# Expert rows of the last two experts: quarter-row gathers and 32x32 transposes on VectorE in place of TensorE's turns

## The chip, the cores and the metric

The kernel runs on one core of a Trainium2 chip. The metric is device time in microseconds of one execution, lower is better. Before the change the median of 3 runs is 857.68 us (857.0 to 857.93). The core has five engines with a queue of their own each, which run their instructions in order and wait for each other through semaphores: TensorE (PE; PEld is its weight load), VectorE (DVE), ScalarE (ACT), GpSimd (POOL) and SyncE (SP), which issues DMAs. Matmuls write to PSUM, from where VectorE or ScalarE take the results.

## The reference

Attention with a sigmoid in place of the softmax gives x; then a mixture of experts with a fixed capacity, in which each token goes to one expert of 8.

```python
scores = scale * np.matmul(q, k.transpose(0, 1, 3, 2)) - np.log(S)   # q, k, v: 8 x 12 x 448 x 64
attn = 1.0 / (1.0 + np.exp(-scores))
x = np.matmul(attn, v) ...                                           # as 3584 tokens x 768
logits = x @ w_gate                                                  # 768 x 8
# (token, expert) pairs in descending order of logit; a token takes the first
# expert that still has room; an expert takes 448 tokens
for e in range(E):
    mask = assigned == e
    h = np.maximum(x[mask] @ w1[e], 0.0)                             # 448x768 @ 768x1024
    out[mask] = h @ w2[e]                                            # 448x1024 @ 1024x768
```

## The kernel before

**Stages.** The attention part comes first (to about 300 us) and writes x to DRAM (`xs`). Then the eight experts follow one another, in the order in which the routing finds them; they are counted 0 to 7 here. Each expert has 448 tokens, in four blocks of 128, 128, 128 and 64 rows.

**Precision.** Matrix products run on a type of 32 bits that TensorE multiplies fast but rounded, so every operand is split into a rounded part and a rest (`wh`, `wl` for weights; `xh`, `xl` for rows; two halves of `hb` and `hr` for h), and three matmuls are added where one would do.

**An expert** (`moe`, a generator that yields after each matmul):
- the *first product*, 144 matmuls of 448 columns (L811 to L815): four quarters, each of two weight units. After each quarter ScalarE writes h twice, rounded (L821, `hb`, `hr`) and in full (L824, `h0`, which has two buffers), and GpSimd subtracts the one from the other (L827);
- the *second product*, 176 matmuls of 384 columns (L856), in two halves of four weight units each. ScalarE copies results out (L771 to L783), GpSimd adds a rest (L784), and after the second half four indirect DMAs on GpSimd's queue (L757) scatter rows to the output.

**Weights** come in 16 units per expert (units 0 to 127 in all): SyncE loads a unit (L698 for w1, L702 for w2, four buffers) three units ahead, ScalarE rounds it (L709), and a subtraction (L711) gives the rest, two units ahead. It runs on GpSimd, and for odd units from 96 on (experts 6 and 7) on VectorE.

**Rows.** A list (`listed`, tile `r_idx`) holds an expert's tokens. Four indirect DMAs on GpSimd's queue gather the rows into `xr` (L731). A *turn* (`xturn`) is then three 128x128 transposes on TensorE per half of the features (L745), ScalarE's rounded copy `xh` (L748) and VectorE's rest `xl` (L749). The first product of the next expert needs all of `xh` and `xl`.

**Routing** (`Router`) runs on VectorE beside the products: a search over bits for an expert's threshold (L178 to L287), a pick, then `place` (two matmuls, L333 and L334, on a running sum r_tot) and `lists` (a one-hot comparison L352, 32 matmuls L360, a cast L377, two matmuls L381, a conversion to the index tile L383). It takes place from expert 0 up to the second product of expert 5.

**Order.** It is written out by hand. A clock adds a cost in ns for each matmul (189 in the first product, 164 in the second); the loop over `moe(kx)` calls the next piece of routing or the first entry of a list of chores (gathers, turns, scatters: a due time each, a last expert by which it has to be done) when its time has come, with 1000 ns between two chores. `flush` issues at an expert's end, one behind another, all chores that are due by then. The order in which pieces are issued is the order in each engine's queue.

Of the kernel before, what the change touches and what calls it, by code (L numbers as in the profile page):

```python
# [21 lines left out]
XR_BUFS = 8  # L22
# [16 lines left out]
HOLD_NS = 600  # L39
H_POOL = 8  # L40
EARLY = 2
FIRST = 4000.0
W_DVE = 96

# [10 lines left out]
def route_consts(nc, cp, K):  # L55
# [47 lines left out]
    nc.vector.tensor_copy(t7, t5)  # L103
    nc.vector.tensor_scalar(K.SEL, t6, t7, None, OP.is_equal)
    K.kk = cp.tile([128, 16, 3], I32, name="c_kk")
    g = 0
# [14 lines left out]
class Router:  # L121
# [219 lines left out]

    def lists(self, alone):

# [36 lines left out]
        for h in range(2):  # L380
            nc.tensor.matmul(p[64 * h:64 * h + 64, :4], bt, K.SEL[:, h, :], start=True, stop=True)  # L381
# [28 lines left out]
    def phase(self, k):  # L410
        if k:
            self.remove()
        if k < 7:
            if k:
                yield T_KEY
                yield from self.keys()
            yield T_KT if k else T_KEYS
            yield from self.search(k == 0)
            yield T_KAP
            self.pick()  # L420
        else:
            self.left()
        yield T_PICK
        self.place(k == 0)
        yield from self.lists(k == 0)


def moe_attention(tc, q, k, v, w_gate, w1, w2, out):
# [7 lines left out]
    with contextlib.ExitStack() as ctx:  # L436
# [213 lines left out]
        late.pop(0)()  # L650
        picked, listed = {}, {}

        def routing():
            for kx in range(E):
                for t in R.phase(kx):
                    if kx not in picked and R.ei is not None:
                        picked[kx] = R.ei
                    yield t
                listed[kx] = R.idx
                R.ei = None  # L660
                yield 0
# [24 lines left out]
        def load_w(u, behind=False):  # L686
# [8 lines left out]
            if st == 0:  # L695
                t = t.rearrange("p (a f) -> p a f", a=3)
                src = w1[ds(gate[kx], 1)].rearrange("e (a p) f -> p (e a) f", p=128)
                nc.sync.dma_start(t, src[:, 3 * j:3 * j + 3, i * 256:(i + 1) * 256])  # L698
            else:
                t = t.rearrange("p (a f) -> p a f", a=2)  # L700
                src = w2[ds(gate[kx], 1)].rearrange("e (a p) f -> p (e a) f", p=128)
                nc.sync.dma_start(t, src[:, 2 * j:2 * j + 2, i * 384:(i + 1) * 384])  # L702
            raw[u] = t

        def split_w(u):
# [3 lines left out]
            nc.scalar.activation(hi, raw[u], AF.Copy)  # L709
            eng = nc.vector if u < 2 or (u >= W_DVE and u % 2) else nc.gpsimd  # L710
            eng.tensor_tensor(lo, raw[u], hi.bitcast(F32), OP.subtract)  # L711
# [22 lines left out]
        def xturn(kx, j, n, hf, wide):  # L734
# [13 lines left out]
            nc.scalar.activation(xh[sl], pv, AF.Copy)  # L748
            nc.vector.tensor_tensor(xl[sl], pv, xh[sl].bitcast(F32), OP.subtract)  # L749

        scat, chores = [], []
# [133 lines left out]
        for kx in range(E):  # L885
            turned = kx + 1 == E
            start = clock[0]

            def prepare():
                t0 = clock[0]  # L890
                lag = max(5000, min(14000, start + 40000 - t0))
                space = max(TURN_FIRST, min(TURN_NS, (start + EXPERT_NS - t0 - lag - 1000) // 4))
                for j, n in blocks():
# [22 lines left out]
            for step, cost in enumerate(moe(kx)):  # L916
# [56 lines left out]
```

## Time and profile before

| | |
|---|---|
| median of the runs | 857.68 us |
| the profiled execution | 857.27 us |
| its span, first to last instruction | 855.5 us |
| expert 5, first matmul to that of expert 6 | 67.16 us (659.08 to 726.24) |
| expert 6 | 62.81 us (726.24 to 789.05) |
| expert 7 up to its last matmul | 60.55 us (789.05 to 849.60) |
| turns on TensorE (L745) | 192 transposes |

All times of the profile come from one execution and are counted from its first instruction. A line of the page or of a view names the source line, the engine, the operation, the tile written and the tiles read, with their shapes; "idle before" is the time in which that engine did nothing ahead of the instruction, and behind the arrow stands what it waited for. "issue" means that it waited for nothing that the profile shows. The chain that ended last is followed back from the end, so its pieces are those which set the time.

### The profile page before, as it was taken

Reading aid. Unit: us, or ns where it says so; the run is one execution under the profiler, and the core shown is the slowest. Engines: PE = TensorE matmul, PEld = TensorE weight load, DVE = VectorE, ACT = ScalarE, POOL = GpSimd, SP = SyncE. Lnnn points to the kernel's source line nnn. Section 1 sums busy time; section 2 is a strip of 40 time slices with the busy share of each in tenths; the row PEclk is TensorE's granted clock in tenths of the full one; section 3 lists DMA queues with packets and bytes.
Section 4 is the critical chain, followed back from the end, with each engine's and each line's share of the span. In section 5 each row is a group of like instructions: output and inputs, shape, how many; then the busy total and the mean of one; then the engine's idle time right before and its main releaser. Section 6 shows DMA issues by size and latency. Waiting matters only on the chain.

```text
span 855.5 us, 16407 instructions
## 1 busy us (share of the span) xinstructions
PE 817.9 (96%) x5517; PEld 650.2 (76%) x5517; DVE 538.9 (63%) x2069; ACT 437.9 (51%) x603; POOL 484.4 (57%) x506
## 2 busy tenths in 40 slices
PE   6999999999999839999999999999999999999997
PEld 3455455454554728999988999999999989999996
DVE  4565555565554989977978969969879852321211
ACT  6777777778775833425424434434434424443332
POOL 9545444445410014867866866876875885743753
PEclk9999999999999978999999999999999999999999
DMA  9776666656530975345435353453553554443331
GB/s 177 153 153 128 131 129 130 124 118 138 121 65 2 318 254 158 111 138 175 114 106 170 115 147 131 147 169 101 157 166 103 156 156 161 139 129 112 129 103 64
DMA packets 196532, 117.58 MB, mean 137 GB/s; under 512 B 145248, under 2 KB 186208, under 8 KB 196448
## 3 DMA queue, kind: packets, MB, share of 16 engines
q1 hardware_dynamic: 183840, 83.30, 37.6%
q0 software_dynamic: 10752, 33.02, 12.6%
q8 instruction: 43, 0.70, 0.4%
q10 hardware_dynamic: 1856, 0.23, 0.2%
q14 instruction: 41, 0.34, 0.1%
HBM read 94.47 MB, written 22.02 MB: 136 GB/s over the span
## 4 chain that ended last, share of the span: by engine, by line
PE 85%; DVE 10%; issue 2%; DMA 1%; ACT 0%; POOL 0%; ACTq 0%; POOLq 0%; SPq 0%; DVEq 0%
PE sc L856 26%; PE tp L559 13%; PE sc L535 12%; PE sc L811 8%; PE sc L815 8%; PE sc L813 8%; DVE r_junk L178 4%; PE tp L565 3%; PE tp L745 2%; PE sc L545 2%; PE tp L580 1%; PE rt L360 1%; DVE r_j L272 1%; DVE r_T L281 1%; DMA xr<-xs,r_idx 1%
## 5 line engine op out<-in xcount | busy, mean ns | idle before, releaser
L711 POOL TENSOR_TENSOR wl<-wr,wh 128x768 fp32r<-128x768 f32 x110 | 202.3, 1855 | 28.3 <-ACT wh L709 28.0
L856 PE MATMUL sc<-wh,hb 128*128 128x384 f32 x768 | 199.8, 338 | 0.0
L525 ACT ACTIVATE at<-sc,bias 128x896 f32<-128x896 f32 x168 | 160.8, 1004 | 62.2 <-PE sc L545 37.8
L466 POOL DMA_DIRECT2D nkq<-in_q_dram x188 | 118.2, 640 | 114.5 <-DVE kqT L510 109.3
L813 PE MATMUL sc<-xl,wh 128*128 128x448 f32 (+2 forms) x396 | 144.2, 364 | 0.0
L811 PE MATMUL sc<-xh,wh 128*128 128x448 f32 (+2 forms) x396 | 144.2, 364 | 0.0
L815 PE MATMUL sc<-xh,wl 128*128 128x448 f32 (+2 forms) x396 | 143.9, 363 | 0.0
L856 PEld LDWEIGHTS sc<-wh,hb 128*128 128x128 f32 x768 | 138.3, 188 | 1.7 <-issue 0.6
L856 PE MATMUL sc<-wl,hb 128*128 128x384 f32 x384 | 130.8, 341 | 0.0
L709 ACT ACTIVATE wh<-wr 128x768 fp32r<-128x768 f32 x128 | 104.0, 850 | 50.9 <-PE sc L856 29.9
L178 DVE TENSOR_SCALAR_CACHE_REDUCE r_junk<-r_KE,r_T 128x224 bf16<-128x224 f32 x315 | 123.3, 442 | 0.1
L559 PE MATMUL tp<-at,nv 128*64 128x448 f32 x576 | 118.6, 548 | 0.0
L821 ACT ACTIVATE hb<-sc 128x768 fp32r<-128x768 f32 x32 | 26.0, 813 | 134.0 <-PE sc L815 134.0
L519 DVE TENSOR_TENSOR kqL<-kqT,kqH 128x896 fp32r<-128x896 f32 (+1 forms) x49 | 52.5, 1072 | 57.8 <-ACT kqH L517 57.7
L827 POOL TENSOR_TENSOR hb<-h,hb 128x768 fp32r<-128x768 f32 x32 | 59.1, 1848 | 50.4 <-ACT h L824 50.4
L559 PEld LDWEIGHTS tp<-at,nv 128*64 128x64 f32 x576 | 37.1, 136 | 59.4 <-issue 57.1
L813 PEld LDWEIGHTS sc<-xl,wh 128*128 128x128 f32 x396 | 74.6, 188 | 6.9 <-DVE xl L749 0.2
L815 PEld LDWEIGHTS sc<-xh,wl 128*128 128x128 f32 x396 | 74.6, 188 | 6.8 <-issue 0.2
L811 PEld LDWEIGHTS sc<-xh,wh 128*128 128x128 f32 x396 | 74.6, 188 | 6.6
L711 DVE TENSOR_TENSOR wl<-wr,wh 128x768 fp32r<-128x768 f32 x18 | 24.0, 1332 | 82.1 <-ACT wh L709 82.0
L856 PEld LDWEIGHTS sc<-wl,hb 128*128 128x128 f32 x384 | 72.2, 188 | 1.8 <-issue 1.0
L535 PE MATMUL sc<-kqH 64*128 64x448 f32 x288 | 59.8, 412 | 6.9 <-ACT kqH L517 6.9
(185 smaller groups left out, 1232.8 us busy)
## 6 DMA issues: line engine op xcount, KB each, us to landing
wr<-in_moe_w_dram SPq DMA_DIRECT2D x128, 384.0 KB, 3.3
xs<-xr SPq DMA_DIRECT2D x32, 336.0 KB, 4.7
nkq<-in_k_dram SPq DMA_DIRECT2D x190, 56.0 KB, 2.5
nkq<-in_q_dram POOLq DMA_DIRECT2D x188, 56.0 KB, 2.6
nv<-in_v_dram SPq DMA_DIRECT2D x94, 96.0 KB, 2.5
nr<-in_v_dram SPq DMA_DIRECT2D x48, 32.0 KB, 2.2
xr<-xs,r_idx POOLq DMA_INDIRECT x32, 4.6
out_dram<-yr,r_idx POOLq DMA_INDIRECT x32, 3.6
```

The costliest lines, as they stand in the source:

```text
L178: nc.vector.tensor_scalar(junk[:, a:b], self.KE[:, a:b], T[:, i:i + 1].bitcast(F32), None, OP.is_ge, OP.add, accum_out=cnt[:, i:i + 1])
L466: qn.dma_start(t[o:o + 32, n], rws[x])
L525: nc.scalar.activation(a, p[:, :, :S], AF.Sigmoid, bias=bias, scale=1 / math.sqrt(D))
L535: nc.tensor.matmul(p[:, j, :S], R[half, c * 128:(c + 1) * 128], M[half], start=i == 0, stop=i == 2)
L559: nc.tensor.matmul(p[j * 64:j * 64 + 64, :S], nat["v", b, g][:, h0 + j, c, :], AT[b, pr, c][:, j, :], start=(c == 0), stop=(c == 2 and pr ...
L709: nc.scalar.activation(hi, raw[u], AF.Copy)
L711: eng.tensor_tensor(lo, raw[u], hi.bitcast(F32), OP.subtract)
L811: nc.tensor.matmul(ph[:, f, lo:hi], wh[:, a, fs], xh[:, dd, lo:hi], start=st, stop=False)
L813: nc.tensor.matmul(ph[:, f, lo:hi], wh[:, a, fs], xl[:, dd, lo:hi], start=False, stop=False)
L815: nc.tensor.matmul(ph[:, f, lo:hi], wl[:, a, fs], xh[:, dd, lo:hi], start=False, stop=en)
L827: nc.gpsimd.tensor_tensor(h2, h0[:, :, t], h1.bitcast(F32), OP.subtract)
L856: nc.tensor.matmul(o, hs, w[:, a], start=st and n == 0, stop=en and n == len(terms) - 1)
```

## The change

For experts 6 and 7 (`BY_DVE`) the rows are not turned on TensorE any more.
- `lists` makes a second index tile `idq` for them: 8 small matmuls (L398) with a selection constant bring tokens to 32-partition groups, and one VectorE operation (L405) makes token * 4 + group of it.
- `gather_quarters` (L783): a gather fetches 128 quarter rows of 192 features: partition 32 g + r gets quarter g of token r of a group of 32 tokens. There are 14 gathers for an expert where there were 4.
- `vturn` (L794): VectorE's 32x32 block transposes, 128 x 384 at a time, write into PSUM what TensorE's transposes wrote; the copies to `xh` and `xl` stay. Feature 192 g + 32 a + w then stands on partition 32 g + w in chunk a, so the w1 rows are loaded in that order, by four DMAs of 32 partitions (L726).
- `FETCH` and `VTURN` set start and spacing of these chores. The turns of expert 6 are due from 7000 ns after its list on, those of expert 7 from 31000 ns after the start of expert 6, in its second product.
- The weight subtraction runs on VectorE for all units from 91 on (the fourth unit of the second product of expert 5).
- Two constants are made early (`SELG`, `gq`).

```diff
+BY_DVE = 6
+FETCH = {6: (0, 1000), 7: (18000, 2500)}
+VTURN = {6: (7000, 3800), 7: (31000, 3000)}
-W_DVE = 96
+W_DVE = lambda u: u >= 91
...
+        if quarters:
+            for u in range(2):
+                for g in range(4):
+                    nc.tensor.matmul(p[32 * g:32 * g + 32, 8 + 8 * u:16 + 8 * u], bt[:, 32 * u:32 * u + 32], K.SELG,
+                                     start=True, stop=True)
         idx = wk.tile([128, 4], I32, name="r_idx", bufs=4)
         nc.vector.tensor_scalar(idx, p[:, :4], 1792.0, None, OP.add)
+        if quarters:
+            self.idq = wk.tile([128, 8, 2], I32, name="r_idq")
+            nc.vector.tensor_scalar(self.idq, p[:, 8:24].rearrange("p (u s) -> p s u", u=2), 4.0, K.gq, OP.mult, OP.add)
...
+                    src = w1[ds(gate[kx], 1)].rearrange("e (g a p) f -> g p (e a) f", g=4, a=ND)
+                    for g in range(4):
+                        nc.sync.dma_start(t[32 * g:32 * g + 32], src[g, :, 3 * j:3 * j + 3, fs])
...
-            eng = nc.vector if u < 2 or (u >= W_DVE and u % 2) else nc.gpsimd
+            eng = nc.vector if u < 2 or W_DVE(u) else nc.gpsimd
...
+        def gather_quarters(kx, s):
+            j, i = s // 4, s % 4
+            if i == 0:
+                xg[kx, j] = xp.tile([128, DM], F32, name="xr", bufs=XR_BUFS)
+            nc.gpsimd.indirect_dma_start(out=xg[kx, j][:, 192 * i:192 * i + 192], out_offset=None,
+                                         in_=xs.rearrange("t (g w) -> (t g) w", g=4),
+                                         in_offset=bass.IndirectOffsetOnAxis(ap=quarter[kx][:, s // 2, s % 2:s % 2 + 1], axis=0))
+        def vturn(kx, j, n, hf):
...
+            p = ps_t.tile([128, 512], F32, name="tp")
+            v = xg[kx, j].rearrange("p (i w) -> p i w", w=192)[:, :n // 32, 96 * hf:96 * hf + 96]
+            nc.vector.transpose(p[:, :3 * n].rearrange("p (a i w) -> p a i w", a=3, w=32),
+                                v.rearrange("p i (a w) -> p a i w", w=32))
...
+            nc.scalar.activation(xh[sl], pv, AF.Copy)
+            return lambda: nc.vector.tensor_tensor(xl[sl], pv, xh[sl].bitcast(F32), OP.subtract)
+        def vturn_block(kx, j, n):
+            for rest in [vturn(kx, j, n, hf) for hf in range(2)]:
+                rest()
...
+            def fetch(e, t, due):
+                if e >= BY_DVE:
+                    for s in range(S // 32):
+                        chores.append((t + FETCH[e][0] + FETCH[e][1] * s, due, lambda s=s: gather_quarters(e, s)))
...
+                if kx + 1 >= BY_DVE:
+                    if kx + 1 not in fetched:
+                        fetch(kx + 1, t0, kx + 1)
+                    for j, n in blocks():
+                        chores.append((t0 + VTURN[kx + 1][0] + VTURN[kx + 1][1] * j, kx + 1,
+                                       lambda j=j, n=n: vturn_block(kx + 1, j, n)))
+                    return
...
-                    for j, n in blocks():
-                        chores.append((t + 1500 * j, kx + 1, lambda j=j, n=n, e=kx + 2: gather(e, j, n)))
+                    fetch(kx + 2, t, kx + 1)
```

What this moves in the queues is seen at three places. A row gives the source line (after, lines behind the top of the file stand lower), the operation, the tile written and those read, the shape, and how many alike stand in a row.

**TensorE, behind the matmuls of the last list** (second product of expert 5; c_SEL and c_SELG are the selection constants, r_bt the cast list). Before:

```order
2786 L856 MATMUL sc<-wh,hb 128x384 x2
2787 L856 MATMUL sc<-wl,hb 128x384
2788 L856 MATMUL sc<-wh,hb 128x384 x2
2789 L381 LDWEIGHTS r_bt
2790 L381 MATMUL rt<-c_SEL,r_bt 64x4
```

After the change:

```order
2803 L910 MATMUL sc<-wl,hb 128x384
2804 L910 MATMUL sc<-wh,hb 128x384 x2
2805 L394 LDWEIGHTS r_bt
2806 L394 MATMUL rt<-c_SEL,r_bt 64x4
2809 L398 LDWEIGHTS r_bt
2810 L398 MATMUL rt<-c_SELG,r_bt 32x8
```

Behind the two matmuls that were there (L381, now L394) stand eight new ones, L398, each with its weight load; the first and the last rows of the stretch are shown. The list of expert 6, at the start of the same product, gets the same eight.

**VectorE, from the one-hot of the last list on** (second product of expert 5; wl is a weight's rest, tp a PSUM tile, xl the rest of the rows). Before:

```order
1318 L352 TENSOR_TENSOR r_oh<-c_io_963,rt 112x2048
1319 L377 CAST r_bt<-rt 128x64
1320 L383 TENSOR_SCALAR r_idx<-rt 128x4
1321 L749 TENSOR_TENSOR xl<-tp,xh 128x3x128 x6
1322 L749 TENSOR_TENSOR xl<-tp,xh 128x3x64 x2
1323 L711 TENSOR_TENSOR wl<-wr,wh 128x768 x3
```

After the change:

```order
1322 L365 TENSOR_TENSOR r_oh<-c_io_1052,rt 112x2048
1323 L739 TENSOR_TENSOR wl<-wr,wh 128x768
1324 L390 CAST r_bt<-rt 128x64
1325 L739 TENSOR_TENSOR wl<-wr,wh 128x768
1326 L401 TENSOR_SCALAR r_idx<-rt 128x4
1327 L405 TENSOR_SCALAR r_idq<-rt,c_gq 128x16
1328 L739 TENSOR_TENSOR wl<-wr,wh 128x768 x2
1329 L794 STREAM_TRANSPOSE tp<-xr 128x384 x2
1330 L799 TENSOR_TENSOR xl<-tp,xh 128x3x128 x2
```

Weight subtractions now stand between the pieces of the list, and the transposes of expert 6 ahead of the subtractions of its rows.

**GpSimd, at the end of expert 5** (yr is a tile of results, out_dram the output, xr the gathered rows). Before:

```order
206 L784 TENSOR_TENSOR yr<-yr,rest 64x384
207 L711 TENSOR_TENSOR wl<-wr,wh 128x768 x3
208 L756 MEMSET spacer 1x1
209 L757 DMA out_dram<-yr,r_idx 3584x768
210 L784 TENSOR_TENSOR yr<-yr,rest 64x384
211 L711 TENSOR_TENSOR wl<-wr,wh 128x768
```

After the change:

```order
198 L739 TENSOR_TENSOR wl<-wr,wh 128x768
199 L783 DMA xr<-xs,r_idq 128x192 x12
200 L838 TENSOR_TENSOR yr<-yr,rest 64x384
201 L783 DMA xr<-xs,r_idq 128x192 x3
202 L838 TENSOR_TENSOR yr<-yr,rest 64x384
203 L783 DMA xr<-xs,r_idq 128x192 x12
204 L810 MEMSET spacer 1x1
205 L811 DMA out_dram<-yr,r_idx 3584x768
```

The weight subtractions are gone from here; the 14 gathers of expert 6 (one stands further up) are followed by 14 of expert 7: two in their own time, 12 from `flush` at the end of expert 5. All four scatters of expert 5 stand behind those 12, and the first h subtraction of expert 6 behind the scatters; before, one scatter stood ahead of the last addition.

More of the change, by code (lines that the diff above doesn't have):

```diff
@@ L104, in route_consts @@
     nc.vector.tensor_scalar(K.SEL, t6, t7, None, OP.is_equal)
+    t11 = cp.tile([128, 8], I32, name="c_t11")
+    nc.gpsimd.iota(t11, [[1, 8]], base=0, channel_multiplier=0)
+    t12 = cp.tile([128, 1], I32, name="c_t12")
+    nc.gpsimd.iota(t12, [[0, 1]], base=32 * 7168, channel_multiplier=1)
+    K.SELG = cp.tile([128, 8], F16, name="c_SELG")
+    nc.vector.tensor_scalar(K.SELG, t11, t7, None, OP.is_equal)
+    nc.vector.tensor_scalar(t12, t12, 5, None, OP.logical_shift_right)
+    K.gq = cp.tile([128, 1], F32, name="c_gq")
+    nc.vector.tensor_copy(K.gq, t12)
+    yield
     K.kk = cp.tile([128, 16, 3], I32, name="c_kk")
@@ L340, in place, with lists @@
         self.sl = sl
-    def lists(self, alone):
+    def lists(self, alone, quarters):
         nc, K, wk, sl = self.nc, self.K, self.wk, self.sl
@@ L424, in phase @@
         self.place(k == 0)
-        yield from self.lists(k == 0)
+        yield from self.lists(k == 0, k >= BY_DVE)
 def moe_attention(tc, q, k, v, w_gate, w1, w2, out):
@@ L650, in moe_attention @@
         late.pop(0)()
-        picked, listed = {}, {}
+        picked, listed, quarter = {}, {}, {}
         def routing():
@@ L659, in routing @@
                 listed[kx] = R.idx
+                quarter[kx] = getattr(R, "idq", None)
                 R.ei = None
@@ L696, in load_w @@
                 t = t.rearrange("p (a f) -> p a f", a=3)
-                src = w1[ds(gate[kx], 1)].rearrange("e (a p) f -> p (e a) f", p=128)
-                nc.sync.dma_start(t, src[:, 3 * j:3 * j + 3, i * 256:(i + 1) * 256])
+                fs = slice(i * 256, (i + 1) * 256)
+                if kx < BY_DVE:
+                    src = w1[ds(gate[kx], 1)].rearrange("e (a p) f -> p (e a) f", p=128)
+                    nc.sync.dma_start(t, src[:, 3 * j:3 * j + 3, fs])
+                else:
+                    src = w1[ds(gate[kx], 1)].rearrange("e (g a p) f -> g p (e a) f", g=4, a=ND)
+                    for g in range(4):
+                        nc.sync.dma_start(t[32 * g:32 * g + 32], src[g, :, 3 * j:3 * j + 3, fs])
             else:
@@ L749, in xturn @@
             nc.vector.tensor_tensor(xl[sl], pv, xh[sl].bitcast(F32), OP.subtract)
+        def gather_quarters(kx, s):
[6 more added lines that the diff above has]
+        def vturn(kx, j, n, hf):
+            if (j, hf) == (0, 0):
+                XH[kx] = (xp.tile([128, ND, S], F32R, name="xh", bufs=2),
+                          xp.tile([128, ND, S], F32R, name="xl", bufs=2))
+            xh, xl = XH[kx]
+            p = ps_t.tile([128, 512], F32, name="tp")
+            v = xg[kx, j].rearrange("p (i w) -> p i w", w=192)[:, :n // 32, 96 * hf:96 * hf + 96]
+            nc.vector.transpose(p[:, :3 * n].rearrange("p (a i w) -> p a i w", a=3, w=32),
+                                v.rearrange("p i (a w) -> p a i w", w=32))
+            pv = p[:, :3 * n].rearrange("p (a t) -> p a t", a=3)
+            sl = (slice(None), slice(hf * 3, hf * 3 + 3), slice(j * 128, j * 128 + n))
+            nc.scalar.activation(xh[sl], pv, AF.Copy)
[3 more added lines that the diff above has]
+                rest()
         scat, chores = [], []
@@ L887, in moe_attention @@
             start = clock[0]
+            def fetch(e, t, due):
+                if e >= BY_DVE:
+                    for s in range(S // 32):
+                        chores.append((t + FETCH[e][0] + FETCH[e][1] * s, due, lambda s=s: gather_quarters(e, s)))
+                else:
+                    for j, n in blocks():
+                        chores.append((t + 1500 * j, due, lambda j=j, n=n: gather(e, j, n)))
             def prepare():
@@ L891, in prepare @@
                 lag = max(5000, min(14000, start + 40000 - t0))
+                if kx + 1 >= BY_DVE:
+                    if kx + 1 not in fetched:
+                        fetch(kx + 1, t0, kx + 1)
+                    for j, n in blocks():
+                        chores.append((t0 + VTURN[kx + 1][0] + VTURN[kx + 1][1] * j, kx + 1,
+                                       lambda j=j, n=n: vturn_block(kx + 1, j, n)))
+                    return
                 space = max(TURN_FIRST, min(TURN_NS, (start + EXPERT_NS - t0 - lag - 1000) // 4))
```

## The prediction

> **What bounds the kernel now.** I read the page's busy shares first, then busy time by stage in the expert part, then the chain that ended last.
>
> ```profile
> PE 817.9 (96%) x5517; PEld 650.2 (76%) x5517; DVE 538.9 (63%) x2069; ACT 437.9 (51%) x603; POOL 484.4 (57%) x506
> ...
> 659.08:726.24 67.16, 66.82 (x419) 62.05 (x418) 37.43 (x162) 26.65 (x44) 50.08 (x42) 1.00 0.50 157
> 726.24:789.05 62.81, 62.81 (x345) 59.73 (x345) 14.43 (x16) 26.76 (x44) 32.76 (x27) 1.00 0.38 123
> ...
> 758.47:789.05 30.58, 30.58 (x177) 30.47 (x177) 5.36 (x4) 11.15 (x16) 12.29 (x9) 1.00 0.36 115
> 789.05:818.80 29.75, 29.75 (x145) 27.04 (x145) 5.96 (x4) 12.66 (x20) 21.07 (x18) 1.00 0.37 126
> ```
>
> A row of a stage gives its from and to, its length, and busy us (and instructions) of PE, PEld, DVE, ACT and POOL, then the granted clock. The first two stages are experts 5 and 6; the last two are a second product (176 matmuls) and a first product (144) with next to nothing between them. TensorE is busy without a gap (62.81 of 62.81 us) at a granted clock of 1.00, while VectorE, ScalarE and GpSimd are less than 55% busy in expert 6. A clean expert costs 29.75 + 30.58 = 60.33 us. Expert 6 takes 62.81, so 2.48 us go to something else on TensorE. The chain that ended last names it:
>
> ```profile
> 707.58 0.66 PE tp L745 x6
> ...
> 710.67 0.66 PE tp L745 x6
> ...
> 714.62 0.65 PE tp L745 x6
> ...
> 718.75 0.52 PE tp L745 x6
> ...
> 741.94 0.66 PE tp L745 x6
> ...
> 746.04 0.66 PE tp L745 x6
> ...
> 749.94 0.65 PE tp L745 x6
> ...
> 754.05 0.51 PE tp L745 x6
> ```
>
> Each row is one block of rows turned on TensorE for the next expert. The first four (during expert 5, for expert 6) add up to 2.49 us, the other four (during expert 6, for expert 7) to 2.48, which is the whole excess of that expert. So these turns lie bare on the engine that sets the end.
>
> **What it removes.** All eight groups, 2.49 + 2.48 = **4.97 us off TensorE**. Nothing else of before is late at these places: product follows product, so the next matmul moves up.
>
> **What it adds on TensorE.** Two lists (experts 6 and 7) get 8 matmuls each of 8 columns (after: L398), directly behind the L381 pair. The trace has no such shape. Its neighbours, in order of time:
>
> ```profile
> 698.91 1.19 PE L360 MATMUL rt<-r_oh,c_mv 112*32 112x64 f16 x32
> 700.04 0.62 PE L856 MATMUL sc<-wh,hb 128*128 128x384 f32 x2
> ...
> 701.11 0.20 PE L381 MATMUL rt<-c_SEL,r_bt 128*64 128x4 f16 x2
> 701.23 0.45 PE L856 MATMUL sc<-wl,hb 128*128 128x384 f32 x1
> ```
>
> 32 matmuls of 64 columns hold TensorE from 698.91 to 700.04, 35 ns each; the pair of 4 columns from 701.11 to 701.23, 60 ns each. So 8 cost 0.28 to 0.48 us, or less, since 8 columns are fewer than 64: half of 0.28 as the lower end. I take the first, which loads weights of 32 columns as the new ones do: 0.28 a list, **+0.6 us** (0.3 to 1.0).
>
> **What it adds to the wait behind the list of expert 6.** VectorE's chain from that list to the sums of the last expert already ends later than TensorE arrives:
>
> ```profile
> 692.90 1.39 DVE L326 TENSOR_TENSOR_SCAN r_tot<-r_mk 112x64 bf16<-112x64 bf16 x1
> 694.21 0.12 DVE L408 CAST r_ei<-csum 1x1 int32<-1x1 f32 x1
> 694.34 0.19 PE L334 MATMUL rt<-r_tot,c_all 112*112 112x63 bf16 x1 [0.30 <-DVE r_ei L408]
> ```
>
> The new index conversion (after: L405; as small as L408, which takes 0.12 us) stands in that chain and reads what the 8 matmuls write. TensorE itself comes 0.28 us later, so the wait grows by some 0.15 and by what the handover costs. Ends: 0 (the scan waits less for GpSimd) and 0.9 (a scan that meets GpSimd anew); I take **+0.4**. Behind the waiting matmul stands the rest of the second product.
>
> **What VectorE takes over.** 16 transposes into PSUM and 21 weight subtractions from GpSimd.
>
> ```profile
> L510 DVE STREAM_TRANSPOSE kqT<-nkq 128x896 f32<-128x896 f32 x47 | 51.9, 1105 | 3.2 <-DMA nkq<-in_k_dram 1.8 <-DMA nkq<-in_q_dram 0.4 <-DMA nv<-in_v_dram 0.2
> L264 DVE STREAM_TRANSPOSE r_ct<-c_CN 128x32 f32<-128x32 f32 x96 | 20.2, 211 | 3.1
> L749 DVE TENSOR_TENSOR xl<-tp,xh 128x384 fp32r<-128x384 f32 x45 | 23.1, 551 | 35.9 <-ACT xh L748 35.8
> ...
> 745.19 0.96 DVE L711 TENSOR_TENSOR wl<-wr,wh 128x768 fp32r<-128x768 f32 x1
> ...
> 710.50 1.00 POOL L784 TENSOR_TENSOR yr<-yr,rest 64x384 f32<-64x384 f32 x1 [0.33 <-ACT yr L783]
> ```
>
> 896 columns cost 1.105 us, so 384 cost about 0.5; the other bound is twelve times the 32-column one, 2.5 us, if the split pattern made every block pay alone. I take 0.55. A full block is then 2 transposes, a ScalarE copy beside the second, and 2 subtractions of 0.55: 2.3 us; a half block 1.3. For expert 6 they come late in expert 5: the four blocks and one subtraction (8.2 + 1.0 us) start when ScalarE has emptied the first half of the second product (710.4 before, 711.4 with the 1.0 us of the two terms above) and a weight copy and a subtraction (0.96 above, 0.85 in the next fence) have followed, about 713.2, and end near 722.4. Expert 6 now starts at 726.24 - 2.49 + 1.0 = 724.7. Cost **0**, with 2.3 us of cover. For expert 7 they stand early in a 30.58 us stage: 0. One subtraction now stands between one-hot and cast of the last list, where VectorE waits for the 1.13 us of L360 anyway; alone it takes 0.96: 0.
>
> **What the gathers do to GpSimd.** 8 gathers become 28; the work taken off is 21 subtractions. What matters is the position. All but one of expert 6's 14 are issued in a row from 697 on (after the h and one weight subtraction, as before), and 12 of the 14 of expert 7 in one go when expert 5 ends, ahead of its 4 scatters and of the first h subtraction of expert 6.
>
> ```profile
> xr<-xs,r_idx POOLq DMA_INDIRECT x32, 4.6
> ...
> L731 POOL DMA_INDIRECT xr<-xs,r_idx x28: 899/960/987, 379.4 to 709.3; - x28
> ...
> 317.06 1.71 POOL L731 DMA_INDIRECT xr<-xs,r_idx  x1 [42.61 <-DMA wr<-in_moe_w_dram]
> 319.07 0.97 POOL L731 DMA_INDIRECT xr<-xs,r_idx  x1 [0.30 <-issue]
> 320.34 0.95 POOL L731 DMA_INDIRECT xr<-xs,r_idx  x1 [0.30 <-issue]
> ...
> 727.82 1.01 POOL L784 TENSOR_TENSOR yr<-yr,rest 64x384 f32<-64x384 f32 x1 [1.18 <-ACT yr L783]
> ...
> 732.63 0.96 POOL L757 DMA_INDIRECT out_dram<-yr,r_idx  x1 [0.21 <-issue]
> ...
> 735.59 1.85 POOL L827 TENSOR_TENSOR hb<-h,hb 128x768 fp32r<-128x768 f32 x1 [0.79 <-ACT h L824]
> ...
> 744.83 0.46 POOL L827 TENSOR_TENSOR hr<-h,hr 128x128 fp32r<-128x128 f32 x1
> ...
> 750.64 0.93 ACT L824 ACTIVATE h<-sc 128x896 f32<-128x896 f32 x1
> 751.44 0.85 ACT L709 ACTIVATE wh<-wr 128x768 fp32r<-128x768 f32 x1
> ```
>
> Gather after gather takes 1.27 us (319.07 to 320.34); a scatter (0.96) with its memset and gap I take at the same. Counted from the start of expert 6: GpSimd is free at 2.6 (728.83), 12 gathers end at 18.0, 4 scatters at 23.1, the first h subtraction (1.85 + 0.46) at 25.4. That one began at 9.4 before (735.59). ScalarE's h of the third quarter goes into a buffer which this subtraction reads (there are two), so it starts at 25.4 and not at 23.1 (750.64, less two blocks of turns); behind it in ScalarE's queue stands the weight copy for the second product (0.80 + 0.85: 27.1), then VectorE's subtraction (0.96: 28.1). TensorE wants it at 29.75. **Cover 1.65 us**, if a quarter gather costs what a whole one does; with it gone the second product waits, microsecond for microsecond.
>
> What may eat it is VectorE's own new work. Of a scatter beside a 128x768 subtraction I found one instance:
>
> ```profile
> 729.24 2.21 DVE L711 TENSOR_TENSOR wl<-wr,wh 128x768 fp32r<-128x768 f32 x1 [7.85 <-ACT wh L709]
> ...
> 730.82 1.50 POOL L757 DMA_INDIRECT out_dram<-yr,r_idx  x1 [0.16 <-issue]
> ```
>
> The scatter took 0.54 more than its neighbours and VectorE ended at 731.45 in the middle of it. Some 5.5 subtractions (one per eighth of a first product, 3.72 us) fall into those 20.3 us: 3.0 us if each does this, a wait of 1.3; none if none does. I take **+0.4**, nearer to none since VectorE's was itself held up by a GpSimd subtraction there, which is gone.
>
> The Trainium skill ("SBUF — State Buffer", section "Who interferes with whom") says that a two-input VectorE operation collides with GpSimd's reads and infers that it leaves descriptor writing alone; by that rule the term is 0 and the sum 0.4 lower, by the row it is 1.3 and the sum 0.9 higher. The 1.50 us above speaks against the rule, weakly, being one instance.
>
> **Loads.** Each w1 unit of experts 6 and 7 is four DMAs.
>
> ```profile
> 730.65 1.19 SPq L698 DMA_DIRECT2D wr<-in_moe_w_dram  x2
> ...
> wr<-in_moe_w_dram SPq DMA_DIRECT2D x128, 384.0 KB, 3.3
> ```
>
> At 0.6 us each, a unit takes 2.4 us of the queue per 3.72 us of product. A unit's buffer comes free some 3.5 units (12.9 us) before ScalarE wants the next data in it; 2.4 + 3.3 us leave 7. Cost 0; without that cover, up to 1.8 us more per unit. The constants (five small operations on GpSimd and VectorE in the attention part, under its matmuls) cost 0, or at worst their own microsecond.
>
> **Sum.** -4.97 + 0.6 + 0.4 + 0.4 = **-3.6 us**. The profiled execution took 857.27 us (span 855.5), so 853.7; the median of the runs is 0.41 higher, which would make 854.1. I say **853.9**. By the terms' ends it goes from 857.27 - 4.97 + 0.3 = 852.6 to 857.27 - 4.97 + 1.0 + 0.9 + 1.3 = 855.5, or 855.9 on the median.
>
> **Rivals.**
>
> A. *The flush is paid in full.* Every subtraction of VectorE holds a gather up for its whole 0.96 us: 5.5 x 0.96 - 1.65 = 3.6 us of wait at the second product of expert 6. For: the 1.50 row. Against: none of 28 gathers took over 0.99, with VectorE busy at other work beside most. Time 857.27 - 4.97 + 1.0 + 3.6 = 856.9.
>
> B. *Slower: a quarter gather costs more than a whole one.* One mechanism, GpSimd's queue at the two bursts. With x us more per gather, expert 6's second product waits 12x - 1.65, and expert 6's start waits 13x - 5.0: 12 gathers from 697.3 end at 712.5, an addition (1.00) stands between, the last one is issued at 713.7 and lands 4.6 later, 718.3, and its half block needs 1.4 more of the time up to 724.7. Both together reach the 4.0 us gained at x = 0.43 (1.7 from gather to gather). At the spacing of the first gather, 2.01 us (317.06 to 319.07, x = 0.74), they are 7.2 + 4.6 = 11.8, and the time is 857.27 - 4.97 + 1.0 + 11.8 = 865.1. Against: the 28 gathers of experts 1 to 7 took 0.90 to 0.99 to issue, with 64 rows or 128, so size should hardly matter.
>
> C. *The transposes cost 2.5 us each*: 13.8 us more for expert 6's blocks, 2.3 covered: 857.27 - 3.6 + 11.5 = 865.2. Against: 896 columns take 1.105.
>
> D. *The turns go and TensorE waits as long for something else*: 857.27 + 1.0 = 858.3. Against: GpSimd, the busiest of the others, has 50.08 of 67.16 us in expert 5 and half of expert 6, and clean products run at 29.75 and 30.58.
>
> **How the numbers follow.** Forecast 0.66; A 0.12 (0.02 faster, 0.10 same); B 0.10; C 0.05 (0.01 same); D 0.03 (same); better than the forecast's lower end 0.04. 0.2% of the time, 1.7 us, is about what a measurement here can tell from no change: faster is below 856.0. Faster 0.66 + 0.02 + 0.04 = 0.72, same 0.10 + 0.01 + 0.03 = 0.14, slower 0.10 + 0.04 = 0.14. The range of 852.4 to 857.6 covers the forecast and A, and leaves out B, C, D and a little below: 0.2.
>
> **What would show it.** Expert 6 at 60.3 to 60.8 us from its first matmul to that of expert 7, and expert 5 at 65.4 to 66, are the forecast. A gap of TensorE at the start of the second product of expert 6, released by wl and behind it by h and GpSimd, is A or B; the gathers' durations tell which. A gap at the start of expert 6 released by xl is C (long transposes) or B (late landings). If the 8 new matmuls of a list take over 0.5 us, their term was wrong.

## The result and the profile after

| | before | after | ratio of after to before |
|---|---|---|---|
| median of the runs | 857.68 us (857.0 to 859.03, 5 runs) | 865.23 us (862.6 to 868.28, 5 runs) | 1.0087 [1.007, 1.0103] |
| the profiled execution | 857.27 us (span 855.5) | 863.38 us (span 861.6) | |

The kernel became slower by 7.5 us where the forecast had it faster by 3.8. The stages of the changed kernel, cut at its own first matmuls (first and second product of expert 5, first and second of expert 6, first of expert 7, and a stretch out of the third row; columns as before):

```profile
659.34:690.98 31.64, 31.60 (x191) 28.08 (x190) 24.85 (x135) 12.83 (x21) 25.86 (x22) 1.00 0.43 132
690.98:726.30 35.32, 33.49 (x228) 31.66 (x221) 22.44 (x45) 14.12 (x24) 23.14 (x20) 1.00 0.46 124
726.30:763.74 37.44, 32.65 (x144) 28.30 (x145) 10.69 (x9) 12.66 (x20) 25.75 (x27) 0.91 0.56 168
763.74:794.35 30.61, 30.61 (x177) 30.51 (x176) 16.09 (x24) 14.37 (x24) 4.49 (x5) 1.00 0.38 112
794.35:824.10 29.75, 29.75 (x145) 27.04 (x145) 11.35 (x8) 12.66 (x20) 14.03 (x14) 1.00 0.47 140
747.80:754.60 6.80, 4.49 (x11) 3.40 (x12) 0.00 (x0) 2.44 (x5) 4.35 (x6) 0.50 0.38 130
```

The second product of expert 6 (30.61) and the first of expert 7 (29.75) are clean, as forecast. The loss is in the third row: a first product with nothing but its 144 matmuls takes 37.44 us in place of 29.75. The last row shows the granted clock at half in 6.80 us of it. TensorE, in order of time at that place:

```profile
740.80 0.36 PE L869 MATMUL sc<-xh,wl 128*128 128x448 f32 x1
...
744.82 0.37 PE L865 MATMUL sc<-xh,wh 128*128 128x448 f32 x1
746.43 0.36 PE L867 MATMUL sc<-xl,wh 128*128 128x448 f32 x1 [1.24 <-issue]
746.64 0.36 PE L869 MATMUL sc<-xh,wl 128*128 128x448 f32 x1
747.16 0.36 PE L865 MATMUL sc<-xh,wh 128*128 128x448 f32 x1 [0.16 <-issue]
749.28 0.53 PE L867 MATMUL sc<-xl,wh 128*128 128x448 f32 x1 [1.76 <-issue]
```

The matmul at 740.80 is the last of the second quarter and adds to the count for which ScalarE waits. After 744.82 TensorE stands still in the middle of a weight unit, where the matmuls that come late wait for no other engine ("issue"). ScalarE beside it:

```profile
735.56 1.59 ACT L737 ACTIVATE wh<-wr 128x768 fp32r<-128x768 f32 x2
752.16 0.81 ACT L875 ACTIVATE hb<-sc 128x768 fp32r<-128x768 f32 x1 [15.00 <-remote]
```

The h of that quarter is made at 752.16, 11.0 us after the matmul ended at 741.16. "Remote" means that the count did arrive just before 752.16, but that no instruction ended just before it. So a finished count of TensorE reached ScalarE 11 us late. GpSimd meanwhile issues the 12 quarter gathers of expert 7, ahead of 4 scatters that run to 749.55:

```profile
729.03 1.50 POOL L783 DMA_INDIRECT xr<-xs,r_idq  x1 [0.15 <-issue]
730.84 0.95 POOL L783 DMA_INDIRECT xr<-xs,r_idq  x1 [0.30 <-issue]
732.09 0.95 POOL L783 DMA_INDIRECT xr<-xs,r_idq  x1 [0.30 <-issue]
...
743.55 0.95 POOL L783 DMA_INDIRECT xr<-xs,r_idq  x1 [0.30 <-issue]
...
748.64 0.91 POOL L811 DMA_INDIRECT out_dram<-yr,r_idx  x1 [0.22 <-issue]
```

The gathers come every 1.25 us, each as dear as a whole-row gather. A smaller loss of the same look lies in the second product of expert 5, beside the row of 12 gathers for expert 6. The chain that ended last, in order of time:

```profile
701.87 6.56 PE sc L910 x29
708.50 2.82 another core or an unknown queue
```

### The profile page after: what moved, and what is told of

Same layout as the page of the kernel before. It is cut to its first block, busy times and chain, and to the rows that moved or that the text cites. A ratio compares the mean times of both kernels' runs of the same rounds, so it can differ in the third digit from the quotient of the medians.

```text
span 861.6 us, 16598 instructions
## 1 busy us (share of the span) xinstructions
PE 817.3 (95%) x5485; PEld 648.0 (75%) x5485; DVE 569.3 (66%) x2111; ACT 438.5 (51%) x603; POOL 468.4 (54%) x507
## 4 chain that ended last, share of the span: by engine, by line
PE 81%; DVE 10%; issue 2%; another core or an unknown queue 2%; DMA 2%; ACT 1%; POOL 0%; SPq 0%; ACTq 0%; POOLq 0%; DVEq 0%
PE sc L910 25%; PE tp L580 13%; PE sc L556 11%; PE sc L869 7%; PE sc L867 7%; PE sc L865 7%; DVE r_junk L191 4%; PE tp L586 2%; PE sc L566 2%; PE tp L773 2%; PE tp L601 1%; PE rt L373 1%; DMA nkq<-in_k_dram 1%; DVE r_j L285 1%
## 5 line engine op out<-in xcount | busy, mean ns | idle before, releaser
L739 POOL TENSOR_TENSOR wl<-wr,wh 128x768 fp32r<-128x768 f32 x89 | 162.6, 1844 | 26.1 <-ACT wh L737 25.8
L739 DVE TENSOR_TENSOR wl<-wr,wh 128x768 fp32r<-128x768 f32 x39 | 47.3, 1241 | 84.1 <-ACT wh L737 84.1
```

## Experiments

The theories, as the expectations name them. T1: a long dense row of gathers holds up what the other engines tell each other. T2: the four w1 loads a unit crowd the DMA engines. T3: plain order on GpSimd, the h subtraction behind the gathers. The runs were made on four chips, called A to D here, and timed side by side with the kernel before, whose median was 857.3 to 858.0 us on each of them. The chip of the changed kernel's first timing is not on record. Each chip was used in one session (A in two), so what differs between chips may also be something that differed between sessions.

### Chip A: what takes the loss away

`a_due_later`:

```diff
-                    fetch(kx + 2, t, kx + 1)
+                    fetch(kx + 2, t, kx + 2)
```

> Only the due of the last expert's quarter gathers is one expert later, so that they are no longer emptied out in one row of 12 at the end of expert 5 but stand in threes between the subtractions of h. Theory T1 (a long unbroken row of quarter gathers holds up what the other engines tell each other: in the changed kernel TensorE's count for quarter 2 of expert 6, whose last matmul ended at 741.2, came at 752.14): the first product of expert 6 is again about 30 us instead of 37.6, the 2 to 3 us at 709 to 712 stay, so 855 to 859 us. T2 (it is the four loads in place of one for a unit of w1 that crowd the DMA engines): 862 to 867, first product of expert 6 still over 35 us. T3 (plain order on GpSimd: the first h subtraction stands behind 12 gathers, the rival A of the prediction): 857 too, but then kernels with single w1 loads and the same row of gathers stay slow.

`b_one_load`:

```diff
-                if kx < BY_DVE:
+                if True:
                     src = w1[ds(gate[kx], 1)].rearrange("e (a p) f -> p (e a) f", p=128)
```

> w1 of experts 6 and 7 is loaded with one DMA a unit as before (its rows then stand in the old order, so what is computed for the last two experts is not the reference's); the quarter gathers and VectorE's transposes stay. T1 and T3: 862 to 867 us and a first product of expert 6 of over 35 us. T2: 853 to 857 us and about 30 us.

`d_whole_rows` (`e_whole_one` has this and the edit of `b_one_load`):

```diff
-                    for s in range(S // 32):
-                        chores.append((t + FETCH[e][0] + FETCH[e][1] * s, due, lambda s=s: gather_quarters(e, s)))
+                    for j, n in blocks():
+                        chores.append((t + FETCH[e][0] + FETCH[e][1] * 4 * j, due, lambda j=j: gather(e, j, 128)))
```

> The 14 quarter gathers of each of the last two experts are 4 gathers of whole rows (what is gathered is not in the order that the 32x32 transposes need, so the last two experts' sums are not the reference's); the four w1 loads a unit, VectorE's transposes and all else stay. T1 and T3: no long row of gathers, so the loss goes: 853 to 856 us, first product of expert 6 30 us. T2: 862 to 867.

> Whole-row gathers and single w1 loads together for the last two experts (sums of these two not the reference's): what is left of the change is the turning on VectorE and the order of the work. All of T1, T2, T3: 853 to 856 us. If it stays above 860, neither gathers nor loads are the cause, but the turning on VectorE or VectorE's wl.

`f_whole_row_burst`:

```diff
-            nc.gpsimd.indirect_dma_start(out=xg[kx, j][:, 192 * i:192 * i + 192], ...
+            nc.gpsimd.indirect_dma_start(out=xg[kx, j], out_offset=None, in_=xs,
+                                         in_offset=bass.IndirectOffsetOnAxis(ap=listed[kx][:, j:j + 1], axis=0))
```

> Every quarter gather of the last two experts is a gather of 128 whole rows into the same buffer (14 an expert, at the same places, four times the bytes; sums of these two experts not the reference's). T1a (it is the unbroken row of gathers, whatever their size): 863 us or more, first product of expert 6 over 36 us. T1b (it is the small pieces of the quarter rows): 853 to 856 us. T3 (order on GpSimd, the h subtraction behind the gathers): as T1a in time, but with TensorE waiting for GpSimd's h only at the second product.

`g_h_on_vector`:

```diff
-H_POOL = 8
+H_POOL = 6
```

> The subtractions of h of experts 6 and 7 are made by VectorE out of the PSUM instead of GpSimd, so that no engine waits for GpSimd behind the row of 12 quarter gathers, which stays where it is. T1 (the row itself holds the others up): 861 to 867 us, first product of expert 6 still over 35 us. T3 (plain order on GpSimd): 853 to 857 us and 29.8 us.

`h_spaced_row` (on top of that):

```diff
+        wide = hp.tile([128, 1024], F32, name="wide", bufs=1)
...
+            if kx == 7:
+                nc.gpsimd.memset(wide, 0.0)
```

> As the kernel with h on VectorE, but GpSimd clears a scratch tile of 128x1024 after each of the last expert's quarter gathers, so that they come every 2.3 us or so instead of every 1.25, in the same unbroken row of 15, with the scatters of expert 5 behind it. T1 with a pace (the gathers are issued faster than what they ask for is worked off): 854 to 858 us, first product of expert 6 about 30 us. T1 by number alone (15 in a row, however far apart): over 861 us.

`m_three_loads` (on top of `a_due_later`):

```diff
-                    for g in range(4):
-                        nc.sync.dma_start(t[32 * g:32 * g + 32], src[g, :, 3 * j:3 * j + 3, fs])
+                    for aa in range(3):
+                        nc.sync.dma_start(t[:, aa], src[:, :, 3 * j + aa, fs])
```

> As the kernel with the last expert's gathers due one expert later (856.04 us), but w1 of the last two experts comes with three DMAs a unit, split by the rows' thirds, instead of four, split by partitions; the same bytes to the same places. If the loads' number adds to the crowding, the 2.2 us of TensorE at 710.38 shrink: 853.5 to 855.5 us. If not: 855 to 857 us.

Measured; the two stages are of the one profiled execution of each kernel, from its first matmul to that of the next stage:

| kernel | second product of expert 5 | first of expert 6 | median (range), us | ratio to before |
|---|---|---|---|---|
| changed kernel, first timing | 35.32 | 37.44 | 865.23 (862.6 to 868.28) | 1.0087 [1.007, 1.0103] |
| `g_h_on_vector` | 37.39 | 36.14 | 865.82 (864.66 to 867.84) | 1.0095 [1.0077, 1.0113] |
| `b_one_load` | 33.83 | 36.23 | 860.71 (859.61 to 862.67) | 1.0035 [1.0022, 1.0048] |
| `a_due_later` | 35.91 | 29.75 | 856.04 (854.9 to 860.11) | 0.9994 [0.9977, 1.001] |
| `m_three_loads` | 39.34 | 29.75 | 862.0 (858.88 to 863.99) | 1.0043 [1.0025, 1.0061] |
| `h_spaced_row` | 41.42 | 29.75 | 859.03 (857.38 to 864.37) | 1.0017 [1.0, 1.0034] |
| `d_whole_rows` | 33.83 | 29.75 | 853.54 (853.35 to 855.15) | 0.9954 [0.9938, 0.9971] |
| `e_whole_one` | 33.84 | 29.75 | 853.43 (852.2 to 854.22) | 0.9946 [0.9928, 0.9963] |

**The quarter gathers carry the whole loss.** With 4 gathers an expert in place of 14 neither stage stalls and the time is 853.5, with four loads or with one (of the 33.83 TensorE waits 0.81 us at L394 for the cast of the last list); T2 alone falls. The loads matter only beside the row: with one load a unit it costs 860.71 - 853.43 = 7.3 us, with four 865.82 - 853.54 = 12.3 (`g_h_on_vector` for the changed kernel, which was not timed on this chip; some 0.9 of it is its own, since its last two second products take 31.05 and 31.21 us for 30.58 and 30.74). In the profiled executions the difference lies in the second product of expert 5, 33.83 against 37.39; in the first product of expert 6 one load loses as much as four. So `b_one_load` met neither of its ranges. Three loads are no better than four: 862.0, against 856.04, and above both ranges of `m_three_loads`.

**It is not the order on GpSimd.** `g_h_on_vector` has no h subtraction on GpSimd, and loses as much. Its ScalarE row is the same one again, 10.4 us after the quarter's last matmul (742.62 to 742.99):

```profile
753.35 0.81 ACT L875 ACTIVATE hb<-sc 128x768 fp32r<-128x768 f32 x1 [15.32 <-remote]
```

So T3 falls as the cause of this loss.

**Breaking the row up, or slowing it, takes away the loss beside it.** In `a_due_later` the gathers of expert 7 stand in threes between subtractions; in `h_spaced_row` they stay one row, but come every 2.08 us:

```profile
739.43 0.95 POOL L784 DMA_INDIRECT xr<-xs,r_idq  x1 [0.16 <-issue]
740.37 0.98 POOL L788 MEMSET wide<- 128x1024 f32 x1
741.51 0.95 POOL L784 DMA_INDIRECT xr<-xs,r_idq  x1 [0.16 <-issue]
```

Both bring the first product of expert 6 to 29.75. The row of expert 6, untouched, goes on costing in the stage before, and by very different amounts: 35.91 and 41.42 in these two, which are alike up to then. Part of that may be the execution that was profiled: with 864.24 us it is 5.2 over the median of `h_spaced_row`, with 855.26 us 0.8 under that of `a_due_later`. The median of `h_spaced_row`, 859.03, is also above the 854 to 858 that it was expected to take. In `h_spaced_row` TensorE stood still twice, and the clock was at half from 713.4 to 723.7:

```profile
712.42 0.62 PE L913 MATMUL sc<-wh,hb 128*128 128x384 f32 x2 [2.05 <-issue]
718.06 1.01 PE L913 MATMUL sc<-wh,hb 128*128 128x384 f32 x2 [2.27 <-ACT yr L840]
```

**`f_whole_row_burst` told nothing of this**: 911.16 us (1.0619 [1.0601, 1.0636]), but its gathers write the same buffer again, so each waits for the one before to land and the row is not dense. Rows came too late for expert 6:

```profile
719.89 0.94 POOL L783 DMA_INDIRECT xr<-xs,r_idx  x1 [3.12 <-DMA xr<-xs,r_idx]
724.11 0.94 POOL L783 DMA_INDIRECT xr<-xs,r_idx  x1 [3.28 <-DMA xr<-xs,r_idx]
```

### Chip B: a row for nobody

`n_row_alone` (on top of `d_whole_rows`; `o_row_of_16_bytes` has 4 columns for 192, `p_row_of_6` 6 gathers for 12, `q_row_of_32_rows` 32 partitions for 128):

```diff
+            if kx == 5:
+                for s in range(12):
+                    nc.gpsimd.indirect_dma_start(out=idle[:128, 192 * (s % 5):192 * (s % 5) + 192], out_offset=None,
+                                                 in_=xs.rearrange("t (g w) -> (t g) w", w=192),
+                                                 in_offset=bass.IndirectOffsetOnAxis(ap=quarter[7][:128, s // 2, s % 2:s % 2 + 1], axis=0))
             flush(kx + 1)
```

> The kernel with whole rows gathered (d_whole_rows, 853.54 us, which loses nothing at this place; sums of experts 6 and 7 not the reference's) plus 12 quarter gathers into a scratch tile that nobody reads, in one row at the end of expert 5. T1 (the row itself): the loss is back, 858 to 864 us, first product of expert 6 33 to 38 us instead of 29.75. If what matters is that the engines wait for what is gathered (buffers, transposes): 853 to 854.5 us, 29.75 us.

> As the kernel with the row alone, but each of the 12 scratch gathers fetches 16 bytes a row instead of 768. T1d (what counts is the issuing, the descriptors of 128 rows one gather after the other): as much lost as with 768 bytes, 858 to 864 us. T1b (it is the bytes that move): 853 to 855 us.

> As the kernel with the row alone, with 6 scratch gathers in place of 12 (a row of 12 with the 3 whole-row gathers and 3 scatters behind them). In the traces so far TensorE first stalls some 12 us after a dense row begins (row from 729.03, stall from about 741 on). T1 with a store that fills over some ten gathers: 853 to 857 us, less than half of the loss with 12. A loss in proportion to the number: 856 to 859 us.

> As the kernel with the row alone, but each scratch gather has 32 rows of 768 bytes in place of 128: a quarter of the descriptors, in the same number of gathers. T1d (descriptors): 853 to 855.5 us. If the number of gathers counts and not their descriptors: as with 128 rows, 858 to 864 us.

| kernel | first product of expert 6 | second of expert 6 | median, us | ratio to before |
|---|---|---|---|---|
| `n_row_alone` | 29.78 | 33.38 | 857.85 | 1.0001 [0.999, 1.0013] |
| `o_row_of_16_bytes` | 29.76 | 34.96 | 857.77 | 1.0004 [0.9992, 1.0017] |
| `q_row_of_32_rows` | 29.75 | 33.38 | 857.52 | 1.0002 [0.9991, 1.0013] |
| `p_row_of_6` | 29.75 | 30.58 | 854.37 | 0.9958 [0.994, 0.9976] |

The times look like T1 with a threshold, and that reading is wrong: no first product stalls. Of the 3.5 us that `n_row_alone` takes over `p_row_of_6`, the profile shows this wait, in the second product:

```profile
749.77 1.86 POOL L882 TENSOR_TENSOR hb<-h,hb 128x768 fp32r<-128x768 f32 x1
751.56 0.48 POOL L882 TENSOR_TENSOR hr<-h,hr 128x128 fp32r<-128x128 f32 x1
...
753.77 0.62 PE L911 MATMUL sc<-wh,hb 128*128 128x384 f32 x2
756.88 0.44 PE L911 MATMUL sc<-wl,hb 128*128 128x384 f32 x1 [2.49 <-DVE wl L740]
```

That is T3, the chain of the prediction's flush: 12 scratch gathers, 3 gathers and 3 scatters stand ahead of the first h subtraction, which ends 28.0 us after the start of expert 6, and h, weight copy and weight subtraction follow. It does not depend on the bytes or the rows of a gather (2.49, 2.48 and 2.50 us with 12), only on their number (none with 6). In `o_row_of_16_bytes` the clock is then at half for 3.4 us, which makes 34.96 out of 33.38. The profiled executions of the other two with 12, 855.87 and 855.79 us, are each the second fastest of ten, so their medians may hold such a stretch as well; that isn't shown. The stall itself did not appear on this chip, so these four say nothing of what it depends on.

### Chips C and D: the changed kernel again

`r_after_again` and `v_after_third` are the changed kernel, `w_due_again` is `a_due_later`. `s_row_scratch_h_vector` is `n_row_alone` with `H_POOL = 6`. `t_last_only`:

```diff
-                if e >= BY_DVE:
+                if e == 6:
+                    for j, n in blocks():
+                        chores.append((t + FETCH[e][0] + FETCH[e][1] * 4 * j, due, lambda j=j: gather(e, j, 128)))
+                elif e == 7:
```

`u_both_spaced` (on top of `a_due_later`):

```diff
+        pause = hp.tile([128, 600], F32, name="pause", bufs=1)
...
+            if kx == 6:
+                nc.gpsimd.memset(pause, 0.0)
```

> The changed kernel as it is, beside the three below on the same chip. 862 to 868 us, with a stall of TensorE inside the first product of expert 6 (over 35 us). If it comes out under 860 with a first product of about 30 us, the stalls depend on the chip, and rows taken on different chips must not be compared.

> The kernel with 12 scratch gathers in a row (n_row_alone, where TensorE waited 2.83 us at the second product of expert 6), with h of experts 6 and 7 on VectorE. If all that the scratch row costs is the wait for h behind it: 853.5 to 855 us. If the row itself costs more (T1): 857 us or more.

> Whole rows for expert 6 (its sums not the reference's), quarter gathers as in the change for expert 7: one dense row of 12 and 4 scatters at the end of expert 5 into the real buffers, none ahead of it. T1 (a dense row of quarter gathers into real buffers is enough): 859 to 863 us, first product of expert 6 over 33 us. If two rows are needed, or the scratch rows showed all that one row does: 854 to 858 us, 29.8 us, with a wait for h at the second product.

> Both rows broken up: the last expert's gathers due one expert later (as in a_due_later, 856.04) and a clearing of a 128x600 scratch tile behind each of expert 6's, so that these come every 1.75 us or so. T1 with a pace: the 2 us at 710 go too, 853 to 855 us, with expert 6 beginning at most 1 us late for the last block's transposes. If 1.75 us are still too dense: 855 to 858 us.

> The changed kernel as it is, on whichever chip. If the stalls belong to the kernel everywhere: 862 to 868 us. If they come with some chips alone: either that, with a first product of expert 6 of over 35 us and counts between the engines missing from the trace, or 853 to 855 us with 29.75 us and none missing; nothing between.

> The kernel with the last expert's gathers due one expert later, beside it. On a chip with stalls: 855 to 858 us, 8 to 10 us under the changed kernel. On a chip without: 852.5 to 854.5 us, within 1 us of the changed kernel (what is left to gain is the 0.2 to 0.5 us that the second product of expert 6 waits there).

| kernel, chip | second product of expert 5 | first of expert 6 | median (range), us | ratio to before |
|---|---|---|---|---|
| `r_after_again`, C | 32.95 | 29.75 | 854.23 (852.88 to 854.5) | 0.996 [0.9946, 0.9974] |
| `s_row_scratch_h_vector`, C | 33.82 | 29.75 | 853.84 (853.08 to 854.42) | 0.9954 [0.9938, 0.9971] |
| `t_last_only`, C | 33.84 | 29.75 | 853.75 (853.14 to 856.11) | 0.9964 [0.995, 0.9978] |
| `u_both_spaced`, C | 37.19 | 29.57 | 857.36 (855.07 to 858.82) | 0.9995 [0.9985, 1.0004] |
| `v_after_third`, D | 36.75 | 37.67 | 865.92 (864.47 to 866.72) | 1.01 [1.0084, 1.0116] |
| `w_due_again`, D | 41.25 | 29.75 | 857.64 (856.44 to 861.53) | 0.9998 [0.9986, 1.0011] |

**The same kernel takes 854.2 us on chip C and 865.9 on chip D**, with nothing between. On C not one stall is left, with the same dense rows at the same pace of 1.25 us; on D and in the first timing both stalls are there. ScalarE's h of the second quarter on chip C, released by that quarter's last matmul:

```profile
738.12 0.81 ACT L875 ACTIVATE hb<-sc 128x768 fp32r<-128x768 f32 x1 [4.19 <-PE sc L869]
```

The same on chip D:

```profile
753.35 0.81 ACT L875 ACTIVATE hb<-sc 128x768 fp32r<-128x768 f32 x1 [15.21 <-remote]
```

So rows of different chips must not be compared without care, as the expectation of `r_after_again` had said. On D, too, the stall beside the row of expert 7 goes when the row is broken up (`w_due_again`, 29.75); its 41.25 are of the slowest of its twelve executions, 861.53 us. `s_row_scratch_h_vector` speaks for the wait for h, and what follows from it, as the whole price of the scratch row, with the reserve that it ran on another chip. `t_last_only` was meant to tell one row from two and can't, on a chip without stalls.

The chips differ in one more thing that the profiles show. In the DMA issues, the last figure is the median time from issue to landing; it is missing where the marks of landings are incomplete. The changed kernel at its first timing:

```profile
xr<-xs,r_idq POOLq DMA_INDIRECT x28
xr<-xs,r_idx POOLq DMA_INDIRECT x24
```

The same kernel on chip C:

```profile
xr<-xs,r_idq POOLq DMA_INDIRECT x28, 3.6
xr<-xs,r_idx POOLq DMA_INDIRECT x24, 4.5
```

Counted over the whole trace, the changed kernel's 825 DMAs should leave 16 marks each, 13200: there are 12235 at the first timing, 12240 on chip D and 13199 on chip C. On chip A every kernel lacks some, from 301 (`e_whole_one`, no stall) to 1070 (`m_three_loads`); on chips B and C none lacks more than 11. The one trace of the kernel before, whose chip isn't on record either, lacks none of its 12112. The changed kernel's first trace has 964 marks fewer than that of chip C, 697 of them in the two stages in which it stalls (second product of expert 5 and first of expert 6, 442 marks for 1139). Marks of counts between the engines are missing too: 566 of TensorE's where chip C has 577. So the stall came only where marks are lost, and there only beside dense rows; that the one causes the other isn't shown. Each timed execution has its span and clock on record too, so the runs can't tell whether the recording takes part in the stall: that rival is untested.

`u_both_spaced` shows why pauses on GpSimd are no free cure (chip C, so without stalls). Its first clearing, of 0.61 us, pushes an h subtraction of expert 5 onto VectorE's running sum, which takes 3.78 us in place of 1.11, and TensorE waits for it; the clock was then at half for 3.4 us. So its 857.36 us lie in the range that was named for a row still too dense, but for this reason:

```profile
693.14 1.83 POOL L884 TENSOR_TENSOR hb<-h,hb 128x768 fp32r<-128x768 f32 x1
...
693.52 3.78 DVE L339 TENSOR_TENSOR_SCAN r_tot<-r_mk 112x64 bf16<-112x64 bf16 x1
...
697.35 0.19 PE L347 MATMUL rt<-r_tot,c_all 112*112 112x63 bf16 x1 [2.87 <-DVE r_ei L429]
```

The kernel with the last expert's gathers due later is what these runs leave for chips that stall: 8 us under the changed kernel on D, but level with the kernel before. On chip C the changed kernel beats the kernel before by 0.4%. No version that computes the reference was faster than the kernel before on a chip that stalls.

## Why the prediction was wrong, step by step

Chip C shows the terms without the stall. The stages there:

```profile
658.44:690.10 31.66, 31.61 (x191) 28.08 (x190) 24.85 (x133) 12.84 (x21) 25.93 (x22) 1.00 0.43 132
690.10:723.05 32.95, 32.79 (x228) 31.90 (x221) 21.57 (x45) 14.24 (x24) 23.44 (x20) 1.00 0.50 137
723.05:752.80 29.75, 29.75 (x145) 27.03 (x145) 8.17 (x7) 12.79 (x20) 23.60 (x27) 1.00 0.59 187
752.80:783.83 31.03, 30.82 (x177) 30.48 (x176) 17.89 (x26) 14.24 (x24) 5.48 (x6) 1.00 0.42 128
```

- **The turns, -4.97.** Held. Expert 6 has no excess of 2.48 any more: 29.75 + 31.03 = 60.78, inside the 60.3 to 60.8 named as the forecast's sign.
- **The flush, +0.4.** Held. The second product of expert 6 takes 31.03 in place of 30.58, +0.45. The first h subtraction starts 23.3 us into the expert (23.1 by the prediction), and TensorE's wait is released by VectorE's wl, as the prediction's chain has it:

```profile
746.38 1.85 POOL L881 TENSOR_TENSOR hb<-h,hb 128x768 fp32r<-128x768 f32 x1
...
753.53 0.45 PE L910 MATMUL sc<-wl,hb 128*128 128x384 f32 x1 [0.21 <-DVE wl L739]
```

- **The 8 matmuls of a list, +0.6, and the wait behind the list of expert 6, +0.4.** Both too dear, and just outside the ends given (0.3 to 1.0 and 0 to 0.9). From start to start the 16 new matmuls hold TensorE 0.29 us in all, and the pairs of place 0.38 + 0.08 where they were 0.52 + 0.08 before. Expert 5 takes 31.66 + 32.95 = 64.61, 0.8 under the 65.4 named.
- **Transposes and gathers by themselves.** Held: 0.55 us a transpose of 384 columns, 0.95 a gather, every 1.25.
- **The sum.** 857.27 - 852.88 = 4.4 us gained in chip C's profiled execution where 3.6 were forecast; its median of 854.23 is 0.3 above the 853.9, and 3.6 below the 857.8 of the kernel before beside it.

**The step that failed is "What the gathers do to GpSimd"**, which counted the two rows as time of GpSimd and of those queued behind it, and nothing else; the bound of the flush (0 to 1.3) and rival A (856.9) share that. On chips A and D and in the first timing the rows also hold back TensorE and ScalarE where these wait for nothing of GpSimd. In the first timing that is 37.44 - 29.75 = 7.7 us in the first product of expert 6, and 35.32 - 32.95 = 2.4 against chip C in the second of expert 5, together 10.1 where the two profiled executions are 863.38 - 852.88 = 10.5 us apart. Of the 7.7, the half clock over 6.80 us is at most 3.4; it came once TensorE had stood still. The numbers of rival B (865.1) and of the time measured agree by chance: its mechanism, dearer gathers, isn't there, and neither is its gap at the second product of expert 6, which in that profile is clean (30.61). Rival D had the kind, a new wait in place of the turns, and argued it away from the shares of busy time, which can't show it. The trace of before has at most four gathers in a row at this pace (from 317.06, 379.42 and 445.88) and scatters in rows of three, so it held no row of 12 to bound it by; the range should have said so.

That a dense row must be there for the stall is shown on chip A (whole rows, threes, 2.08 us apart: no stall beside them) and for threes on D; that it is not enough, on chip C. Why a count arrives late, and why on some chips alone, stays open; so does the number of gathers from which it begins, and whether it needs one row or two.

## What to carry to other kernels

Splitting a gather in four is not free, because each piece costs as much to issue as the whole: a row of 12 puts everything behind it on GpSimd 15 us later, and, on some chips, stalls engines that do not wait for it. Spread such issues between other work of the queue, and time them on more than one chip and in more than one session when the gain is under 1%. When a wait is released by "remote" or "issue" and the producer had long ended, look at what else is issued at that time rather than at the two engines.

## What the runs showed of the hardware beyond that

- After stalls of TensorE its clock was at half for 3.4 us (`u_both_spaced`), 6.8 (changed kernel) or 10.2 (`h_spaced_row`), multiples of 3.4. The Trainium skill ("TensorE: Matmul & The Clock Gate", Part 1) gives an idle window of about 3.4 us for the drop to half rate; the lengths agree with a window of that size, but it was not idle here. In the 3.41 us ahead of the drop TensorE was busy for 1.73 us in the changed kernel (744.39 to 747.80), 0.55 in `u_both_spaced` and 1.36 in `h_spaced_row`.
- A gather beside VectorE's two-input work can take longer: 1.50, 1.14, 1.22 and 1.12 us beside a weight subtraction (changed kernel at 729.03, 737.09, 701.28 and 702.80) and 2.77 beside the one-hot comparison of a list and the subtraction behind it (at 698.20), against 0.95 alone. Not every one does: on chip C the gather at 734.02 took 0.99 beside two subtractions (733.24 to 735.06). The Trainium skill ("SBUF — State Buffer", section "Who interferes with whom") infers that such operations leave descriptor writing alone; the longer rows speak against it, as the one scatter of the prediction did.
